# Stored attention tails in two halves, and filling products ahead of the closing stage, in a four-layer interleaved network

## The chip, the cores and the metric

The kernel runs on one core of one Trainium2 chip, as one launch. The metric is the device time of that launch in microseconds (us); lower is better. The engines are named as in the profile: PE is TensorE (matrix products; PEld its weight loads), DVE is VectorE, ACT is ScalarE, POOL is GpSimd and SP is SyncE, which here only issues transfers. An engine name with a q (SPq) is the issue of a transfer by that engine.

## The reference, cut to what matters

Four layers, A B A B, each added to its input. Layer A is a recurrent attention with a memory of 8 tokens over 64 segments of 32 tokens: each segment's first 8 output rows are the memory of the next one, so the segments form a chain. Layer B is a linear attention with learned feature maps, over all 2048 tokens.

```python
def _A_ref(x, mem0, Wq, Wk, Wv, Wo, seg_len):       # x: 1 x 2048 x 640, 32 heads of 192, memory of 8
    mem = mem0
    for s in range(n_seg):                           # 64 segments of 32 tokens
        h = concatenate([mem, x[:, 32*s:32*s+32]])
        q, k, v = h @ Wq, h @ Wk, h @ Wv
        p = softmax(where(mask, q @ k.T * scale, -1e9))
        o = (p @ v) @ Wo
        mem = o[:, :8]
        outs.append(o[:, 8:])

def _B_ref(x, wqkv, w_phi, wo):                      # 32 heads of 20
    q, k, v = split(x @ wqkv)
    phi_q = cat(softmax(q @ w_phi), softmax(-q @ w_phi)); phi_k likewise
    kv, z = phi_k.T @ v, phi_k.sum(tokens)
    return (phi_q @ kv / (phi_q @ z + 1e-6)) @ wo

x = x + _A_ref(layernorm(x), ...); x = x + _B_ref(layernorm(x), ...)   # twice
```

## The kernel before

Layer A is computed in three parts. `A_pre` computes what does not depend on the memory. `A_chain` walks the 64 segments in order, and in each of them four rounds of eight heads (forwards in even segments, backwards in odd ones, `rounds(s)`); its order on every engine is as written. Only the rows that the memory needs go through the output projection inside the chain (`wo_round`, L1263, into the PSUM tile `ps_w`). The last 8 tokens of each segment, its "tail", are not projected there: `turn_tail` lays out a pair of rounds, and `store_tail` (L1256) stores it to `otb_d` in DRAM. A segment stores two such tails of 128 x 192 elements, the one of rounds 0 and 1 and the one of rounds 2 and 3.

The third part is the closing stage, at the beginning of layer B. There the tails of 16 segments at a time (`tb` = 0 to 3) are fetched (`fetch_tails`, L1471), spread into the order that a product needs (`spread_tails`: for each round two copies, by DVE (L94) or ACT (L96) as the letters in `engines` say), and multiplied with all of Wo (`multiply`: 48 steps of a product of 512 columns into `kv_ps[tb % 2]`, L1506, and one of 128 columns into `ps_post`, L1507). Step c uses round c // 12. The results are copied to `obB` by DVE (L1509) and ACT (L1510) and stored (L1512). `kv_ps` has a bank for each of two neighbouring products, but `ps_post` has one bank for all (the pool with `bufs=1`), so the second product's first step on `ps_post` waits for ACT's copy of the first.

The fetches of `tb` 0 and 1 are requested in the chain's last segment, in the list `held`, which `release` issues: four pieces of Wo, the fetch of `tb` 0, four more pieces of Wo (L797), and the fetch of `tb` 1. `tb` 0 is spread inside the chain: rounds 0 and 1 by DVE ahead of its last steps (`"vv"`), rounds 2 and 3 by ACT behind the chain (`"  ss"`). The fetches of `tb` 2 and 3 reuse the memory of 0 and 1 and are issued in layer B, after `wqkv` (L545) and four blocks of rows of x (L406). All of these are on SP's queue, and a transfer there uses one of eight semaphores in turn, so that it also waits for the landing of the eighth transfer before it.

In layer B a scheduler orders each engine's instructions; ACT and DVE then work strictly in that order. In the first layer B the weights are also fused (`fuse`, products and transposes into the four banks `ps_t` and `ps_f`) between the steps of `multiply`. Below, "the first place" is the passage from the first chain to the first layer B (about 1330 to 1360 us), and "the second place" that from the second chain to the second layer B (about 2910 to 2940 us).

Of the kernel before, what the change touches and what calls it, by code (L numbers as in the profile page):

```python
# [8 lines left out]
P = 128  # L9
BF16 = mybir.dt.bfloat16  # L10
# [112 lines left out]
class Kernel:  # L123
# [180 lines left out]
    def layer_B(self, x_dram, at_dram, xout_dram, xnext_dram, li, bp, post):  # L304


        nc, tc, KC, D = self.nc, self.tc, self.KC, self.Dm
# [6 lines left out]
        at = 0  # L314
# [17 lines left out]
        at = LATE  # L332
# [14 lines left out]
        with tc.tile_pool(name=f"B{li}_kv", bufs=1, space=bass.MemoryType.PSUM, reuse_waits="tile") as kvp, \  # L347
# [5 lines left out]
            def side_bank(name):  # L353
                return ptp.tile([P, 512], F32, name=name, tag="side")

            nc.gpsimd.memset(wbd[:], 0.0)
            for i in range(HC):
                n = len(range(i, H, HC))
                nc.gpsimd.dma_start(out=wbd[DH * i:DH * i + DH, 0:n, DH * i:DH * i + DH],
                                    in_=self.B_w_phi[i:H:HC].rearrange("h d f -> d h f"))  # L360
# [190 lines left out]
            with tc.issue_after(last.ins):  # L551
                nc.sync.dma_start(out=wqkv[:, :, 2 * D:3 * D],
                                  in_=self.B_wqkv.rearrange("(k p) n -> p k n", p=P)[:, :, 2 * D:3 * D])
            multiply(0, ow[0], kv_ps[0], side_bank("ps_post"), {})
            ow.append(spread(2, ot[2]))
            side = []
# [144 lines left out]
    def layer_A(self, xn_dram, at_dram, li, x_raw=None):  # L701
# [5 lines left out]
        self.kqb_d = dram.tile([NR, P, NSEG, 192], BF16, name=f"kqb{li}")  # L707
        self.vb_d = dram.tile([NSEG // 8, NR, 2, 64, 2, 2 * VH], BF16, name=f"vb{li}")
        self.tails_d = dram.tile([NSEG // 8, 8, 8, self.Dm], BF16, name=f"tails{li}")
        self.otb_d = dram.tile([P, NSEG, 384], BF16, name=f"otb{li}")  # L710
        wview = self.wview
        wov = self.A_Wo.rearrange("h d m -> (h d) m").rearrange("(q j f) m -> q f j m", j=6, f=32)
        low = self.view(0, LATE)
# [9 lines left out]
        at = 2 * own  # L723
# [63 lines left out]
        def load_both(r, last):  # L787
            for c in (*range(1280, both, 1280), 0):
                held.append(lambda c=c: load_piece(wo_both, r, c))
            if last:  # L790
                held.append(lambda: self.keep_tails(0, low))
                for c in (*range(1280, both, 1280), 0):
                    held.append(lambda c=c: load_piece(wo_kept, order_first, c))
                held.append(lambda: self.keep_tails(1, low))

        def load_piece(into, r, c):
            self.last_load = nc.sync.dma_start(out=into[:, c:c + 1280], in_=self.wo_rows[r, :, own + c:own + c + 1280])  # L797
            return self.last_load
# [259 lines left out]
    def A_chain(self, xn_dram, at_dram, li, load_slot, piece, late_wo, load_both, wo, low):  # L1058
# [3 lines left out]
        with tc.tile_pool(name=f"A{li}_ch", reuse_waits="tile", bufs=1) as sp, \  # L1062
# [190 lines left out]
                return otb[:]  # L1253

            def store_tail(otb, s, r):
                nc.gpsimd.dma_start(out=self.otb_d[:, s, 192 * (r // 2):192 * (r // 2) + 192], in_=otb)  # L1256

            def wo_round(W, r, OT, first, last, part=range(12)):
                for i in part:
# [70 lines left out]
            for s in range(NSEG):  # L1330
# [55 lines left out]
                for n in range(L):  # L1386
                    raw = q_or_k("Q", n + 1)
                    if n == 2:
                        otb = turn_tail(otr)
                    E = weigh()  # L1390
                    next_kq(s, n)
                    turn_rows(raw)
                    if n == 1:
                        step = wo_round(W, order[0], OTs[0], True, False, range(OWN, 12))
                        if s == NSEG - 1:
                            load_both(order[L], True)
                            self.kept_tails = []
                            self.release(step, 12)
                            tails = self.kept_tails
                        else:  # L1400
                            load_both(order[L], False)
                    raw = q_or_k("K", n + 1, n + 1 == L)
                    O = attend(E, n)
                    if n != 2:
                        tails_after(n)
                    fetch_kq(s, n)
                    if n == 2:
                        store_tail(otb, s, order[1])
                    rc = weigh_rows(O)
                    if n == 1:  # L1410
                        rct = weigh_tail()
                    turn_rows(raw)
                    if n == L - 1:
                        output_steps(STEPS[0])
                    pv = v_banks()
                    project(hT, pv, "V", n + 1, s, range(KC))
                    if s == 0 and n == 1:
                        late_wo(1)
                        late_wo(2)
                    osc = raw_of["Q"][:, 0:384]  # L1420
                    for G in range(2):
                        scaled(osc[:, 192 * G:192 * G + 192], O, rc, G, "s")
                    turn(n, osc)
                    v_rows(pv, n + 1, "sv")
                    if n == 1:
                        otr = tail_rows(rct, raw_of["K"][:, 0:192])
# [38 lines left out]
        self.kept_tails.append(self.fetch_tails(tb, low))  # L1465
        return self.tails_load

    def fetch_tails(self, tb, low):
        o = 7680 + 12288 * (tb % 2)
        ot = low[:, o:o + 6144].rearrange("p (s f) -> p s f", f=384)  # L1470
        self.tails_load = self.nc.sync.dma_start(out=ot, in_=self.otb_d[:, 16 * tb:16 * tb + 16, :])  # L1471
        return ot

    def spread_tails(self, tb, ot, low, engines="vsvs"):
        o = 7680 + 12288 * (tb % 2)
        ow = low[:, o + 6144:o + 12288].rearrange("p (r j s x) -> p r j s x", r=4, j=6, x=16)
        for r in range(4):
            if engines[r:r + 1] in ("", " "):
                continue
            for b in range(2):  # L1480
                at = 192 * (r // 2) + (0 if (r + b) % 2 else 16)
                o = ow[:, r, :, b:16:2, :]
                i = ot[:, b:16:2, at:at + 16]
                i = ap3(i, [list(i.ap[0]), [32, 6], *[list(d) for d in i.ap[1:]]])
                self.ev.copy(out=o, in_=i, eng=engines[r])
        return ow

    def post_steps(self, ops):

        nc = self.nc  # L1490
        at_dram, wo, low = self.post_args

        def fetch(tb):
            return self.fetch_tails(tb, low)

        def spread(tb, ot):
            return self.spread_tails(tb, ot, low)

        def multiply(tb, ow, p0, p1, between):
            for c in range(48):  # L1500
                if c in between:
                    between[c]()
                G, j = c % 12 // 6, c % 6
                lhsT = ow[:, c // 12, j, :, :].rearrange("p s x -> p (s x)")[:, G:2 * P:2]
                w = wo[c // 12, c % 12]
                nc.tensor.matmul(p0[:, :], lhsT=lhsT, rhs=w[:, 0:512], start=(c == 0), stop=(c == 47))  # L1506
                nc.tensor.matmul(p1[:, 0:128], lhsT=lhsT, rhs=w[:, 512:640], start=(c == 0), stop=(c == 47))  # L1507
            ob = ops.tile([P, 640], BF16, name="obB", tag="obB", bufs=2)
            done = (nc.vector.tensor_copy(out=ob[:, 0:512], in_=p0[:, :]),  # L1509
                    nc.scalar.activation(out=ob[:, 512:640], in_=p1[:, 0:128], func=ACT.Copy))  # L1510
            av = at_dram.rearrange("(s t) d -> s t d", t=32)
            nc.sync.dma_start(out=av[16 * tb:16 * tb + 16, 24:32, :], in_=ob[:, :])  # L1512
            return done

        return fetch, spread, multiply
# [35 lines left out]
```

## Time and profile before

| | |
|---|---|
| median of 3 runs | 3170.55 us (3170.22 to 3171.96) |
| profiled execution | 3169.9 us, of which the span from first to last instruction 3168.0 us |
| mean granted TensorE clock | 0.992 |
| busy | PE 95%, DVE 69%, ACT 60%, POOL 44% of the span |
| DMA | 749.67 MB, mean 237 GB/s |

In the rows of a timeline the columns are the start, the time of the group, the engine, the line, the operation with output and inputs, the number of instructions, and in brackets the idle time of the engine before it and what ended that. In the rows of the stretches the columns are the stretch and its length, the busy time of PE, PEld, DVE, ACT and POOL, the granted TensorE clock, the mean busy share of the DMA engines and the bytes moved per second.

### The profile page before, as it was taken

What the parts mean: (1) busy time and instruction counts of PE and PEld (TensorE: products, weight loads), DVE (VectorE), ACT (ScalarE), POOL (GpSimd) and SP (SyncE); (2) the same over time, 40 slices, a digit from 0 to 9 for tenths busy, and PEclk for the clock granted to TensorE, in tenths of its full rate; (3) what the DMA queues carried; (4) which work ended last, traced back from release to release, by engine and by line L of the source; (5) the groups of instructions that cost most, each with busy time, mean ns of one, the idle gap of its engine ahead of it and who ended that gap; (6) DMA issues with size and microseconds to landing.
All of it is one profiled execution on the core that took longest, in us unless ns stands there. A gap on an engine that the chain in (4) does not pass through costs nothing.

```text
span 3168.0 us, 141538 instructions
## 1 busy us (share of the span) xinstructions
PE 2993.8 (95%) x59586; PEld 1920.6 (61%) x59586; DVE 2184.4 (69%) x5426; ACT 1906.3 (60%) x4536; POOL 1392.8 (44%) x2872
## 2 busy tenths in 40 slices
PE   8789999999999999899999999999999999998999
PEld 7656666666666665555377566666666666665553
DVE  5467777777777777656644677777777777776565
ACT  3356666666666666646433566666666666666453
POOL 3255555555555555430122555555555555554300
PEclk9999999999999999999999999999999999999999
DMA  9977777877877877840268777777877777778300
GB/s 377 340 263 257 261 248 251 265 257 250 272 252 251 267 256 246 288 166 1 103 246 320 257 255 246 263 264 245 264 259 249 255 261 255 246 259 287 130 1 34
DMA packets 338873, 749.67 MB, mean 237 GB/s; under 512 B 68874, under 2 KB 115330, under 8 KB 335166
## 3 DMA queue, kind: packets, MB, share of 16 engines
q1 hardware_dynamic: 267998, 636.89, 58.3%
q0 software_dynamic: 69376, 100.10, 10.9%
q8 instruction: 469, 7.68, 1.0%
q10 hardware_dynamic: 864, 3.64, 0.3%
q14 instruction: 166, 1.36, 0.1%
HBM read 670.77 MB, written 78.01 MB: 236 GB/s over the span
## 4 chain that ended last, share of the span: by engine, by line
PE 76%; DVE 8%; DMA 6%; issue 5%; ACT 3%; POOL 2%; ACTq 0%; DVEq 0%; SPq 0%; POOLq 0%
PE ps_qk_k L1154 13%; PE ps_qk_q L1154 13%; PE ps_v L1154 12%; PE ps_w L1263 11%; PE ps_s L1191 6%; PE ps_pre L985 4%; PE ps_o L1204 3%; PE kv L1506 2%; DVE raws L1453 2%; ACT raws L1234 2%; DVE hT L1455 2%; PE ps_pq L517 2%; PE ps_t L1217 1%; PE ps_wo L466 1%; DVE QK L1377 1%
## 5 line engine op out<-in xcount | busy, mean ns | idle before, releaser
L1154 PEld LDWEIGHTS <-hT 128*32 128x32 bf16 x30720 | 787.1, 96 | 461.0 <-DVE hT L1455 78.7
L1174 DVE STREAM_TRANSPOSE QK<-raws 128x512 bf16<-128x512 bf16 (+1 forms) x1152 | 730.0, 642 | 219.3 <-ACT raws L1169 163.7
L1130 POOL COPY QK<-kqb 64x192 bf16<-64x192 bf16 x1024 | 349.5, 341 | 486.6 <-PE ps_s L1191 254.1
L1154 PE MATMUL ps_qk_q<-arena,hT 128*32 128x384 bf16 x10240 | 511.3, 327 | 41.4 <-DVE hT L1455 25.6
L1154 PE MATMUL ps_qk_k<-arena,hT 128*32 128x384 bf16 x10240 | 510.1, 328 | 3.0 <-ACT E L1273 1.4
L1169 ACT ACTIVATE raws<-ps_qk_k 128x512 bf16<-128x512 f32 (+1 forms) x640 | 313.5, 510 | 254.0 <-PE ps_qk_k L1154 243.5
L1234 ACT ACTIVATE raws<-ps_o,under 128x192 bf16<-128x192 f32 x1024 | 373.8, 420 | 121.9 <-DVE under L1228 102.5
L1154 PE MATMUL ps_v<-arena,hT 128*32 128x384 bf16 x8192 | 428.4, 326 | 4.0 <-issue 3.0
L1169 ACT ACTIVATE raws<-ps_qk_q 128x512 bf16<-128x512 f32 x512 | 305.7, 597 | 166.6 <-PE ps_qk_q L1154 153.1
L1134 POOL DMA_DIRECT2D Vp<-vb x512 | 257.9, 504 | 316.6 <-PE ps_t L1217 210.7
L1123 POOL DMA_DIRECT2D kqb<-kqb x512 | 292.4, 571 | 69.7 <-POOL QK L1130 59.4
L1191 PEld LDWEIGHTS <-QK 128*80 128x80 bf16 x4096 | 196.0, 121 | 184.9 <-issue 153.8
L1183 DVE CAST Vp<-ps_v 64x384 bf16<-64x384 f32 x512 | 286.3, 559 | 24.5 <-ACT Vp L1181 8.7
L1263 PE MATMUL ps_w<-arena,under 128*32 128x320 bf16 x6144 | 280.6, 300 | 9.5 <-DMA arena<-wo_rows 4.1
L1191 PE MATMUL ps_s<-QK 128*80 128x80 bf16 x4096 | 253.4, 209 | 21.8 <-POOL QK L1130 13.6
L1181 ACT ACTIVATE Vp<-ps_v 64x384 bf16<-64x384 f32 x512 | 246.4, 481 | 35.1 <-PE ps_v L1154 33.6
L1273 ACT ACTIVATE E<-ps_s 80x320 bf16<-80x320 f32 x512 | 217.7, 425 | 42.8 <-PE ps_t L1217 28.6
L985 PEld LDWEIGHTS <-arena 128*128 128x128 bf16 x1920 | 187.9, 98 | 31.0 <-issue 4.7
L1119 POOL DMA_DIRECT2D attn<-under x128 | 91.3, 713 | 262.0 <-DVE under L1115 223.5
L1112 ACT ACTIVATE raws<-ps_w 64x160 f32<-64x160 f32 x256 | 76.6, 299 | 201.1 <-DVE raws L1453 199.6
L1204 PE MATMUL ps_o<-Vp,E 80*32 80x193 bf16 x4096 | 180.3, 248 | 10.2 <-issue 5.7
L1263 PEld LDWEIGHTS <-under 128*32 128x32 bf16 x6144 | 147.2, 96 | 41.6 <-issue 9.8
(167 smaller groups left out, 4360.5 us busy)
## 6 DMA issues: line engine op xcount, KB each, us to landing
arena<-wo_rows SPq DMA_DIRECT2D x560, 320.0 KB, 4.8
arena<-in_A_Wq_dram SPq DMA_DIRECT2D x427, 384.0 KB, 4.5
arena<-in_A_Wk_dram SPq DMA_DIRECT2D x298, 384.0 KB, 5.6
arena<-in_A_Wv_dram SPq DMA_DIRECT2D x290, 384.0 KB, 5.9
kqb<-kqb POOLq DMA_DIRECT2D x512, 48.0 KB, 4.3
kqb<-arena POOLq DMA_DIRECT2D x14, 1536.0 KB, 9.7
Vp<-vb POOLq DMA_DIRECT2D x512, 24.2 KB, 3.8
otb<-otb POOLq DMA_DIRECT2D x256, 48.0 KB, 4.0
```

The costliest lines, as they stand in the source:

```text
L985: nc.tensor.matmul(ps[:, T * i:T * i + T], lhsT=w[b][:, P * c:P * c + P], rhs=xBT[:, b, :], start=(b == 0), stop=(b == KC - 1))
L1123: nc.gpsimd.dma_start(out=kqb[:], in_=self.kqb_d[r, :, s, :])
L1130: nc.gpsimd.tensor_copy(out=o, in_=kqb[h, :].rearrange("p (x c q) -> p x c q", c=3, q=16))
L1134: nc.gpsimd.dma_start(out=Vs[n % 2][64:80, :], in_=self.vb_d[s // 8, r].rearrange("g (t s) x f -> s (g t) (x f)", s=8)[s % 8])
L1154: last = nc.tensor.matmul(o, lhsT=hT[:, b, :], rhs=rhs, start=(i == 0), stop=(i == KC - 1), tile_position=(0, 32 * g), skip_group_check=True)
L1169: nc.scalar.activation(out=raw[:, c], in_=ps[:, c], func=ACT.Copy)
L1174: nc.vector.transpose(out=o, in_=i)
L1183: nc.vector.tensor_copy(out=o, in_=i)
L1191: nc.tensor.matmul(S[0:80, c0:c0 + 80], lhsT=KT[:, 4 * x + c, :], rhs=QT[:, 4 * x + c, :], start=(c % 2 == 0), stop=(c % 2 == 1), skip_gro ...
L1204: nc.tensor.matmul(O[G][32 * h:32 * h + 32, VH * G:VH * G + 193], lhsT=E[0:80, 80 * h + 32 * G:80 * h + 32 * G + 32], rhs=V[0:80, VH * h:V ...
L1234: nc.scalar.activation(out=out, in_=i, func=ACT.Copy, scale=rc[G])
L1263: step = nc.tensor.matmul(W[q:q + 32, 0:320], lhsT=OT[i // 6][:, i % 6 // 2, 32 * (i % 2):32 * (i % 2) + 32], rhs=rhs, start=(first and i ...
```

## The change

The tails in DRAM get an outer dimension for the pair of rounds, so that the tails of one pair for 16 segments lie together, and each fetch becomes two transfers, one for each pair, with a semaphore each. Nothing of the stores but their address changes. Rounds 0 and 1 (or 2 and 3) of a spread depend on their own half alone. At the closing stage's beginning, PE gets 16 products of the identity matrix with the Wo rows of round 1, 512 columns each, into `kv_ps[0]`, whose result is overwritten by the first real product.

```diff
@@ layer_B
                 nc.sync.dma_start(out=wqkv[:, :, 2 * D:3 * D], ...)
+            for _ in range(16):
+                nc.tensor.matmul(kv_ps[0][:, :], lhsT=self.ident[:, :], rhs=self.post_args[1][1, 0][:, 0:512], start=True, stop=True,
+                                 skip_group_check=True)
             multiply(0, ow[0], kv_ps[0], side_bank("ps_post"), {})
@@ layer_A
-        self.otb_d = dram.tile([P, NSEG, 384], BF16, name=f"otb{li}")
+        self.otb_d = dram.tile([2, P, NSEG, 192], BF16, name=f"otb{li}")
...
             if last:
+                held.append(lambda: self.fetch_half(0, 0, low))
                 held.append(lambda: self.keep_tails(0, low))
                 for c in (*range(1280, both, 1280), 0):
                     held.append(lambda c=c: load_piece(wo_kept, order_first, c))
+                held.append(lambda: self.fetch_half(1, 0, low))
                 held.append(lambda: self.keep_tails(1, low))
@@ A_chain
             def store_tail(otb, s, r):
-                nc.gpsimd.dma_start(out=self.otb_d[:, s, 192 * (r // 2):192 * (r // 2) + 192], in_=otb)
+                nc.gpsimd.dma_start(out=self.otb_d[r // 2, :, s, :], in_=otb)
...
-                            self.release(step, 12)
+                            self.release(step, 14)
@@
-    def fetch_tails(self, tb, low):
+    def fetch_half(self, tb, g, low):
+        o = 7680 + 12288 * (tb % 2) + 3072 * g
+        ot = low[:, o:o + 3072].rearrange("p (s f) -> p s f", f=192)
+        self.tails_load = self.nc.sync.dma_start(out=ot, in_=self.otb_d[g, :, 16 * tb:16 * tb + 16, :])
+        return self.tails_load
+
+    def fetch_tails(self, tb, low, halves=(1,)):
         o = 7680 + 12288 * (tb % 2)
-        ot = low[:, o:o + 6144].rearrange("p (s f) -> p s f", f=384)
-        self.tails_load = self.nc.sync.dma_start(out=ot, in_=self.otb_d[:, 16 * tb:16 * tb + 16, :])
-        return ot
+        for g in halves:
+            self.fetch_half(tb, g, low)
+        return low[:, o:o + 6144].rearrange("p (g s f) -> p g s f", g=2, f=192)
...
-                at = 192 * (r // 2) + (0 if (r + b) % 2 else 16)
+                at = 0 if (r + b) % 2 else 16
...
-                i = ot[:, b:16:2, at:at + 16]
+                i = ot[:, r // 2, b:16:2, at:at + 16]
...
-            return self.fetch_tails(tb, low)
+            return self.fetch_tails(tb, low, (0, 1))
```

## The prediction

> **What bounds the kernel now.** I read the page first: how busy PE is, and what the chain of work that ended last consists of.
>
> ```profile
> span 3168.0 us, 141538 instructions
> PE 2993.8 (95%) x59586; PEld 1920.6 (61%) x59586; DVE 2184.4 (69%) x5426; ACT 1906.3 (60%) x4536; POOL 1392.8 (44%) x2872
> PE 76%; DVE 8%; DMA 6%; issue 5%; ACT 3%; POOL 2%; ACTq 0%; DVEq 0%; SPq 0%; POOLq 0%
> ```
>
> PE is busy for 95% of the span and is 76% of that chain, so a change pays only where it fills a hole of PE or speeds PE up. Next I asked for stretches of 4 us around the two places where a chain ends and layer B begins.
>
> ```profile
> 1332.00:1336.00 4.00, 3.26 (x88) 1.79 (x77) 1.50 (x5) 1.16 (x3) 2.88 (x6) 1.00 1.06 397
> 1336.00:1340.00 4.00, 0.00 (x0) 0.00 (x0) 0.53 (x2) 0.00 (x0) 0.00 (x0) 0.88 1.01 348
> 1340.00:1344.00 4.00, 3.84 (x15) 1.92 (x16) 1.72 (x7) 3.13 (x6) 1.31 (x2) 0.50 1.06 434
> 1344.00:1348.00 4.00, 4.00 (x24) 2.02 (x23) 1.17 (x4) 2.65 (x5) 0.00 (x0) 0.77 1.01 348
> 1352.00:1356.00 4.00, 4.00 (x33) 2.23 (x31) 0.00 (x0) 0.00 (x0) 0.66 (x4) 1.00 1.00 422
> 2920.00:2924.00 4.00, 2.95 (x22) 1.66 (x23) 2.25 (x8) 2.24 (x5) 0.68 (x2) 1.00 1.05 424
> 2932.00:2936.00 4.00, 4.00 (x31) 2.18 (x29) 0.69 (x1) 0.28 (x1) 0.00 (x0) 1.00 1.02 419
> ```
>
> At the first place PE has no work from 1336 to 1340, and then works at a granted clock of 0.50 and 0.77. At the second place the clock stays 1.00. The DMA engines are full (1.0 or more) in all these stretches. The timeline of the first place shows what PE waits for.
>
> ```profile
> 1329.28 0.32 SPq L1471 DMA_DIRECT2D arena<-otb  x1
> 1335.22 0.58 PE L1263 MATMUL ps_w<-arena,QK 128*32 128x320 bf16 x10 [0.33 <-issue]
> 1339.36 6.10 SPq L406 DMA_DIRECT2D arena<-in_A_x_dram  x4
> 1339.47 1.17 DVE L94 COPY arena<-arena 128x768 bf16<-128x768 bf16 x4 [5.04 <-DMA arena<-otb]
> 1340.16 0.61 PE L1506 MATMUL kv<-arena 128*128 128x512 bf16 x1 [4.36 <-DVE arena L94]
> 1341.89 3.04 ACT L96 ACTIVATE arena<-arena 128x768 bf16<-128x768 bf16 x4
> 1345.70 3.97 SPq L1471 DMA_DIRECT2D arena<-otb  x2
> 1356.18 0.28 ACT L1510 ACTIVATE obB<-ps_post 128x128 bf16<-128x128 f32 x1 [6.86 <-PE ps_post L1507]
> 1356.51 0.27 PE L1507 MATMUL ps_post<-arena 128*128 128x128 bf16 x2
> ```
>
> The fetch of the first 16 tails, requested at 1329.28, ends DVE's wait at 1339.47, and DVE's copies end PE's 4.36 us. The next two fetches are issued from 1345.70. The first product ends at about 1356.2, ACT copies its `ps_post` (1356.18), and the second product's `ps_post` starts at 1356.51, as soon as that bank is free. The second place has the same shape.
>
> ```profile
> 2916.58 1.00 PE L1263 MATMUL ps_w<-arena,QK 128*32 128x320 bf16 x24
> 2920.36 0.90 DVE L94 COPY arena<-arena 128x768 bf16<-128x768 bf16 x3 [4.55 <-DMA arena<-otb]
> 2921.05 0.39 PE L1506 MATMUL kv<-arena 128*128 128x512 bf16 x1 [3.47 <-DVE arena L94]
> 2921.61 0.38 PE L1506 MATMUL kv<-arena 128*128 128x512 bf16 x1
> 2921.88 0.38 PE L1506 MATMUL kv<-arena 128*128 128x512 bf16 x1
> 2926.65 4.14 SPq L1471 DMA_DIRECT2D arena<-otb  x2
> 2934.30 0.28 ACT L1510 ACTIVATE obB<-ps_post 128x128 bf16<-128x128 f32 x1 [3.86 <-PE ps_post L1507]
> 2934.63 0.27 PE L1507 MATMUL ps_post<-arena 128*128 128x128 bf16 x2
> 2937.46 3.04 ACT L96 ACTIVATE arena<-arena 128x768 bf16<-128x768 bf16 x4 [2.88 <-DMA arena<-otb]
> ```
>
> **The halves: when the first product may start.** A fetch is 1536 KB.
>
> ```profile
> arena<-otb SPq DMA_DIRECT2D x4, 1536.0 KB, 10.4
> ```
>
> Half of it is 0.786 MB. The queue is full, so the first half lands earlier by what its other half takes: at the 397 and 348 GB/s of the first place some 2.1 us, so at 1337.4 instead of 1339.5, and two of DVE's four copies (1.17 / 2 = 0.6) make step 0 ready at 1338.0. At the second place, at 424 GB/s, it is 1.9 us: 2918.5, and ready at 2919.1.
>
> **The fillers: when it does start.** Two steps of the warm product stand 0.27 us apart (2921.61, 2921.88) and stream 640 columns; 512 columns are 0.216 us, and 16 of them 3.46 us. As the two programs are built, PE's order is otherwise the same, the fillers stand right behind the chain's last `ps_w` product, and they wait for nothing. At the first place that one ends at 1335.22 + 0.58 = 1335.80, so the fillers end at 1339.26, later than the 1338.0 of the data: the product starts 0.9 us before 1340.16. At the second place 2917.58 + 3.46 = 2921.04, against 2921.05 before: nothing is won there, the fillers take the 1.9 us that the half would have given.
>
> **The clock.** PE's hole of 4.36 us led to half the clock at the first place, the one of 3.47 us at the second did not. In the slow stretches the loss is 3.84 x 0.50 + 4.00 x 0.23 = 2.84 us. With fillers there is no hole, so I take all of it back. [...] The row bears out that the clock fell; that other runs do without is not seen, since all three timed runs are slower than the profiled one and a run without the loss would be 2.84 us faster. I keep 2.84.
>
> So the first product of the first place would end 0.9 + 2.84 = 3.7 us sooner: the second one's `ps_post` could start at 1352.8.
>
> **What is late next: ACT's order.** As built, the changed program has ACT and DVE in another order in layer B. Before, ACT's copy of the first product's `ps_post` (L1510) stands ahead of all copies of `tb` 2. Now the two copies of `tb` 2, round 1, stand ahead of it, at both places; they wait for the first half of the fetch of `tb` 2. Queued behind that wait are L1510, and behind L1510 PE, whose second product needs the one `ps_post` bank, and SP's store of the result. DVE's copy of `kv_ps[0]` is moved behind two such copies as well, but that bank is needed by the third product only, 13 us later; that costs nothing.
>
> When does that half land? Before, the fetch of `tb` 2 was issued at 1345.70, held up by SP's queue (L406 until 1345.46), not by the copies that free its memory (ACT until 1344.93). That queue drains at the rate of the full DMA engines, so I leave the issue there, and the half lands earlier by 0.786 MB at 422 or 419 GB/s, 1.9 us. First place: 1345.70 + 10.4 - 1.9 = 1354.2. Second place: 2937.46 is when ACT got the whole; 2935.6. ACT then needs 3.04 / 2 = 1.52 us for the two copies and 0.28 us for L1510, and PE follows 0.05 us later (1356.46 to 1356.51).
>
> - First place: 1354.2 + 1.52 + 0.28 + 0.05 = 1356.1 against 1356.51. Of the 3.7 us, 0.4 are left.
> - Second place: 2935.6 + 1.85 = 2937.4 against 2934.63: a loss of 2.8 us.
>
> **The rest of the change.** Four more transfers for each layer on SP at 0.32 us each: SP has waits of several us here, and what is behind (rows of x, `wqkv`) is needed only after four products of 13 us. By the eight semaphores, `wqkv` now waits for the two first halves; the queue still holds two Wo pieces and more then, so I see no hole in the DMA. At nothing, with the cover named; if the DMA ran dry for 1 us, all landings above would be 1 us later, 2 us in the sum. The stores of the chain (256, of 384 bytes a row as before) only change address. What slower or faster ones could do in 128 segments no row shows; the bounds are what PE waits for transfers, since these share the engines:
>
> ```profile
> PE ps_w L1263 <- DMA arena<-wo_rows: 8.1, 12, 1.5
> PE ps_qk_q L1154 <- DMA arena<-in_A_Wq_dram: 4.6, 2, 2.9
> PE ps_o L1204 <- DMA Vp<-vb: 1.9, 4, 1.0
> ```
>
> Together 14.6 us, some of it start-up: from -10 (gone) to +10 (doubled). I take zero: same number of rows, same bytes.
>
> **Sum.** -0.4 + 2.8 = +2.4 us on the profiled 3169.9 us (the span of 3168.0 and 1.9 around it), which is 0.65 us under the median of the runs: 3170.55 + 2.4 = 3173.0 us. That is within 0.2% (6.3 us, about what a measurement of this kernel can tell from no change).
>
> **Rivals.**
> 1. *The new stall itself cools the clock (slower).* PE stands still for 1352.8 to 1356.1 = 3.3 us at the first place, 2.8 at the second. Each restart at half the clock costs 2.84 as above. In one place: 3175.9. In both, as it would be if the halves land about 1 us later than I say (+2 more): 2.4 + 5.7 + 2 = +10, and with no later landing +8.1: 3178.7 to 3180.7. It decides from a hole between 3.47 us (clock kept) and 4.36 us (lost). For it: the first place is close to that. Against: the second is well below.
> 2. *No stall.* If the first half of `tb` 2 landed 3 us sooner than I say, ACT would be ready in time, and -3.7 and 0 remain: 3166.8. For it: the half's memory is free sooner than before. Against: SP's queue, not memory, set the issue.
> 3. *The cold clock is rare in ordinary runs of before.* Then the second `ps_post` could start at 1353.7 before, and the first place loses 2.4 instead of winning 0.4: +5.2, 3175.8. Against it speak the three runs, as said.
> 4. *The stores' new addresses slow or speed the chain.* Slower by 10 us: 3180.6; faster by 10: 3160.6. Nothing in the profile speaks for either.
>
> That the change does not do what it says is not open: fillers and halves stand in the built program where they are meant.
>
> **How the numbers follow.** Forecast 0.27, rival 1 in one place 0.10, rival 2 0.09, rival 3 0.08: all within 0.2%, 0.54. Rival 1 in both places 0.21 and rival 4 slower 0.15: slower, 0.36. Rival 4 faster: 0.10. The range from 3166 to 3181 leaves out the faster side of rival 4 and part of its slower one. The forecast's own range is 3171 to 3175, by 1 us of landing time at each place.
>
> **What would show it.** In the changed profile: the clock at 1.00 from 1336 to 1352; the first product starting near 1339.2 and 2921.0, right behind fillers 0.216 us apart; ACT's two copies of `tb` 2 right ahead of L1510's, and a wait of PE for ACT's `obB` of some 3 us at both places, starting near 1352.8 and 2934.2. I am wrong if PE goes through from the first to the second product, if the clock drops there, or if the span of the 64 segments itself differs by more than 1 us.

## The result, and the profile after

The changed kernel took 3178.28 us (median of 17 runs) beside 3170.22 us for the kernel before on the same chip, a ratio of 1.0022 (95% interval 1.0012 to 1.0033): by this ratio +7.0 us, between +3.8 and +10.5. A second comparison, told below, gave 1.0011 (0.9999 to 1.0022). The forecast was +2.4 us, "within 0.2%"; the first measurement lies just above that line, inside the stated range of 3166 to 3181 us and outside the forecast's own of 3171 to 3175. The profiled execution took 3182.34 us.

The page of the changed kernel: busy time, and the chain of work that ended last.

```profile
span 3180.5 us, 141588 instructions
PE 3004.0 (94%) x59584; PEld 1926.7 (61%) x59618; DVE 2185.9 (69%) x5426; ACT 1909.7 (60%) x4536; POOL 1398.5 (44%) x2872
PE 73%; DMA 9%; DVE 8%; issue 4%; ACT 3%; POOL 2%; SPq 0%; DVEq 0%; POOLq 0%; ACTq 0%
```

In that chain DMA has gone from 6% to 9% and PE from 76% to 73%: more of it hangs on transfers. Among the waits of PE stands one that the kernel before does not have (total us, times, longest):

```profile
PE ps_post L1518 <- ACT obB L1521: 8.8, 2, 4.7
```

The product into `ps_post` is L1518 now (L1507 before), ACT's copy of it L1521 (L1510), the product into `kv` L1517, the chain's `ps_w` product L1268, the fetch of tails L1476, the fillers L555 (the trace has 15 of the 16). The timeline of the first place:

```profile
1341.61 0.32 PE L1268 MATMUL ps_w<-arena,QK 128*32 128x320 bf16 x4 [0.16 <-DMA arena<-wo_rows]
1342.09 3.40 PE L555 MATMUL kv<-arena,ident 128*128 128x512 bf16 x15 [0.16 <-issue]
1343.80 2.52 SPq L545 DMA_DIRECT2D arena<-in_B_wqkv_dram  x2
1343.86 1.17 DVE L94 COPY arena<-arena 128x768 bf16<-128x768 bf16 x4 [3.57 <-DMA arena<-otb]
1345.33 0.38 PE L1517 MATMUL kv<-arena 128*128 128x512 bf16 x1
1346.75 5.74 SPq L406 DMA_DIRECT2D arena<-in_A_x_dram  x4
1352.72 5.68 SPq L1476 DMA_DIRECT2D arena<-otb  x4
1361.72 1.57 ACT L96 ACTIVATE arena<-arena 128x768 bf16<-128x768 bf16 x2 [6.63 <-DMA arena<-otb]
1363.32 0.28 ACT L1521 ACTIVATE obB<-ps_post 128x128 bf16<-128x128 f32 x1
1363.65 0.37 PE L1518 MATMUL ps_post<-arena 128*128 128x128 bf16 x2 [4.69 <-ACT obB L1521]
```

The fillers fill the old hole, and the first product starts behind them. Then ACT stands still for the half of `tb` 2 until 1361.72, copies it, only then frees the `ps_post` bank, and PE has stood for 4.69 us. The second place has the same shape:

```profile
2922.94 1.00 PE L1268 MATMUL ps_w<-arena,QK 128*32 128x320 bf16 x24 [0.37 <-DVE QK L1382]
2925.49 1.17 DVE L94 COPY arena<-arena 128x768 bf16<-128x768 bf16 x4 [2.28 <-DMA arena<-otb]
2927.34 0.38 PE L1517 MATMUL kv<-arena 128*128 128x512 bf16 x1
2934.06 5.81 SPq L1476 DMA_DIRECT2D arena<-otb  x4
2943.18 1.58 ACT L96 ACTIVATE arena<-arena 128x768 bf16<-128x768 bf16 x2 [6.48 <-DMA arena<-otb]
2945.11 0.27 PE L1518 MATMUL ps_post<-arena 128*128 128x128 bf16 x2 [4.14 <-ACT obB L1521]
```

The stretches (start and end, length, busy time of PE, PEld, DVE, ACT and POOL, granted clock, DMA share, GB/s) show what follows each stall:

```profile
1342.00:1346.00 4.00, 3.91 (x20) 1.88 (x20) 1.59 (x6) 0.77 (x3) 0.00 (x0) 1.00 1.02 357
1358.00:1362.00 4.00, 0.96 (x6) 0.41 (x5) 0.24 (x1) 0.28 (x1) 0.00 (x0) 1.00 1.03 415
1362.00:1366.00 4.00, 2.35 (x13) 1.46 (x13) 1.80 (x6) 3.75 (x6) 0.00 (x0) 0.54 1.01 395
2942.00:2946.00 4.00, 0.89 (x8) 0.53 (x8) 1.86 (x5) 2.79 (x5) 0.00 (x0) 1.00 1.01 416
2946.00:2950.00 4.00, 4.00 (x19) 1.99 (x18) 0.18 (x1) 0.64 (x1) 0.00 (x0) 0.57 1.04 380
```

At the first place the clock stays 1.00 where it fell before, and falls 20 us later, behind the new stall. At the second place, where it had stayed 1.00, it falls too.

### The profile page after: what moved, and what is told of

Read it like the earlier page. It is cut to its first block, busy times and chain, and to the rows that moved or that the text cites. A ratio compares the mean times of both kernels' runs of the same rounds, so it can differ in the third digit from the quotient of the medians.

```text
span 3180.5 us, 141588 instructions
## 1 busy us (share of the span) xinstructions
PE 3004.0 (94%) x59584; PEld 1926.7 (61%) x59618; DVE 2185.9 (69%) x5426; ACT 1909.7 (60%) x4536; POOL 1398.5 (44%) x2872
## 3 DMA queue, kind: packets, MB, share of 16 engines
q0 software_dynamic: 69376, 100.10, 10.8%
q10 hardware_dynamic: 864, 3.64, 0.3%
## 4 chain that ended last, share of the span: by engine, by line
PE 73%; DMA 9%; DVE 8%; issue 4%; ACT 3%; POOL 2%; SPq 0%; DVEq 0%; POOLq 0%; ACTq 0%
PE ps_qk_k L1159 12%; PE ps_qk_q L1159 12%; PE ps_v L1159 11%; PE ps_w L1268 10%; PE ps_s L1196 6%; PE ps_pre L990 5%; DMA arena<-wo_rows 3%; PE ps_o L1209 2%; DVE raws L1458 2%; PE ps_wo L466 2%; PE kv L1517 2%; DMA under<-tails 2%; ACT raws L1239 2%; PE ps_pq L517 2%; DVE hT L1460 1%
## 5 line engine op out<-in xcount | busy, mean ns | idle before, releaser
L1268 PE MATMUL ps_w<-arena,under 128*32 128x320 bf16 x6144 | 282.7, 301 | 13.0 <-DMA arena<-wo_rows 5.8
L1268 PEld LDWEIGHTS <-under 128*32 128x32 bf16 x6144 | 148.4, 96 | 43.9 <-issue 11.7
```

Source lines behind the costliest of these rows:

```text
L1268: step = nc.tensor.matmul(W[q:q + 32, 0:320], lhsT=OT[i // 6][:, i % 6 // 2, 32 * (i % 2):32 * (i % 2) + 32], rhs=rhs, start=(first and i ...
```

## The experiments

Two theories at the start. **A**: the fillers and the halves do what they should, and the loss is ACT's order, which makes PE wait for the `ps_post` bank and then cools the clock. **Rivals**: B, the fillers cost by themselves; C or D, the halves or the new addresses change the transfers. Every kernel was timed beside the kernel before on the same chip. Its own median was 3170.2, 3171.6, 3177.3 and 3177.8 us in the four comparisons, so ratios are compared.

To see where each kernel stands at the two places, I take from each profiled execution the time from the start of the chain's last `ps_w` product to the start of the last step of the fourth output product, and add the two places: 128.3 us for the kernel before, 137.6 for the changed kernel. "At the places" below is the difference of this sum to 128.3.

| kernel | at the places, us | ratio to before (95%) | us from the ratio |
|---|---|---|---|
| changed | +9.3 | 1.0022 (1.0012 to 1.0033) | +7.0 |
| changed, again | +8.2 | 1.0011 (0.9999 to 1.0022) | +3.5 |
| e1_fill | -1.4 | 1.0003 (0.9989 to 1.0017) | +1.0 |
| e2_halves | -5.2 | 0.9966 (0.9952 to 0.9981) | -10.8 |
| e2_halves, again | -3.0 | 0.9990 (0.9979 to 1.0001) | -3.2 |
| e3_order | -2.6 | 0.9975 (0.9961 to 0.9989) | -7.9 |
| e4_bank | -0.4 | 0.9999 (0.9982 to 1.0016) | -0.3 |
| e5_layout | +2.8 | 0.9992 (0.9980 to 1.0003) | -2.5 |
| e7_warm | +4.6 | 1.0021 (1.0009 to 1.0034) | +6.7 |
| e7_warm, again | +6.7 | 1.0021 (1.0009 to 1.0034) | +6.7 |
| e8_stall | +13.0 | 1.0043 (1.0026 to 1.0059) | +13.6 |
| e9_nine | -4.9 | 0.9978 (0.9965 to 0.9992) | -7.0 |
| e10_stall | +1.0 | 0.9988 (0.9978 to 0.9998) | -3.8 |

The second column is from one execution, the last from the ratio over all runs, whose intervals are about 4 us to each side; they agree within 5.6 us, and what is ordered far apart in one is so in the other. (In the trace of e2_halves the last step into `kv` is missing at the second place; its time is taken from the `ps_post` step behind it, which gives -5.2, where the expectation of its second run says 5.8 us less.) Of the changed kernel's +9.3 us, 5.1 have come about when the second product's `ps_post` starts, and 4.1 come behind it.

**e1_fill: the fillers alone**, on the kernel before (old layout, whole fetches).

```
+            for _ in range(16):
+                nc.tensor.matmul(kv_ps[0][:, :], lhsT=self.ident[:, :], ...)
             multiply(0, ow[0], kv_ps[0], side_bank("ps_post"), {})
```

> The kernel before with the 16 fillers alone (whole fetches, old layout). Theory A (the loss is PE waiting for ps_post behind ACT's copies of tb 2, and the cold clock after that wait): in this build ACT's copy of the first ps_post stays ahead of the copies of tb 2, so there is no wait; the first product starts with its data as before (4.4 us after the chain's last product), the clock stays 1.00 at the first place: -2.8 us there, 0 to +0.2 at the second, about -2.6 us against the kernel before. Rival B (the fillers themselves cost, by power, instruction loading or by delaying PE): slower than before by most of the 7 us that the change costs.

Measured: 1.0003, +1.0 us between -3.5 and +5.4. The fillers alone do not cost 7 us; B is out, and e3_order, with the same fillers, confirms it. The 2.6 us that A let them win are not seen, but they lie inside the interval. The profile has no wait of PE for `obB`, and this is what is left of PE's waits for the first copies:

```profile
PE kv L1509 <- DVE arena L94: 0.8, 1, 0.8
```

**e2_halves: layout and halves, no fillers.**

```
-            for _ in range(16):
-                nc.tensor.matmul(kv_ps[0][:, :], lhsT=self.ident[:, :], ...)
```

> The changed kernel without the fillers: halves and new layout alone. In this build ACT's copy of the first ps_post is ahead of the copies of tb 2 again. Theory A: no wait of PE for obB; the hole of PE ahead of the first product shrinks from 4.4 to about 2.5 us at the first place and from 3.5 to 2.2 at the second, and the clock stays up: -1.9 - 2.8 - 1.3 = about -6 us against the kernel before. Rival C (the halves or the stores' new addresses slow the transfers): slower than before, by up to the 7 us of the whole change, with a longer chain of segments or later landings.

Measured: 0.9966, and 0.9990 in the second comparison. The halves win (the second time with an interval that reaches 1.0001) and cost nothing, so C is out. Without the fillers the scheduler leaves ACT's copy of the first `ps_post` ahead of the copies of `tb` 2: the bad order comes only from both parts of the change together. PE's waits:

```profile
PE ps_post L1515 <- DVE arena L94: 4.3, 2, 2.3
```

The 7.8 us for the first copies (4.36 + 3.47) have become 4.3, and nothing replaces them.

**e3_order: the whole change with ACT's order mended.** The copies of `tb` 2 are issued only after those of the first product's banks.

```
-            multiply(0, ow[0], kv_ps[0], side_bank("ps_post"), {})
-            ow.append(spread(2, ot[2]))
+            done0 = multiply(0, ow[0], kv_ps[0], side_bank("ps_post"), {})
+            with tc.issue_after(done0[0].ins), tc.issue_after(done0[1].ins):
+                ow.append(spread(2, ot[2]))
```

> The changed kernel with one thing put right: the copies of tb 2 are issued behind the copies of the first product's results, so that ACT's copy of the first ps_post is ahead of them. Fillers, halves and layout as in the changed kernel. Theory A: no wait of PE for obB and no cold clock at either place; the first product starts 3.4 us behind the chain's last product (before: 4.4 and 3.5): -1 - 2.8 - 0.1 = about -4 us against the kernel before, 11 us faster than the changed kernel. Rivals B and C: still about 7 us slower than before.

Measured: 0.9975, 11 to 15 us under the changed kernel by the ratios of the two comparisons, with the same fillers, halves and layout. There is no wait for `obB`, and the stretches around the old stall are full at full clock:

```profile
1340.00:1344.00 4.00, 4.00 (x26) 2.09 (x25) 2.07 (x8) 2.79 (x6) 1.23 (x2) 1.00 1.03 378
1352.00:1356.00 4.00, 3.95 (x32) 2.34 (x32) 0.69 (x1) 0.28 (x1) 1.07 (x6) 1.00 1.08 400
1356.00:1360.00 4.00, 4.00 (x37) 2.58 (x36) 1.03 (x4) 1.97 (x3) 0.00 (x0) 1.00 1.00 410
```

**e4_bank: ACT's order left bad, but the second product given a free bank** for its 128 columns, so that it need not wait.

```
-            multiply(1, ow[1], kv_ps[1], side_bank("ps_post"), between[0])
+            multiply(1, ow[1], kv_ps[1], kv_ps[2], between[0])
```

> The changed kernel with ACT's order left as it is (the copies of tb 2 for round 1 ahead of the first ps_post's copy), but the second product's 128 columns go to the third kv bank, which is free at that time. If theory A's link is the ps_post bank: PE goes from the first to the second product without a wait, though ACT's copy is as late as before; clock 1.00; about -4 us against the kernel before. If the late copy costs by another way (SP's store of the first product, the copies of tb 2 late for the third product): a wait of PE somewhere later, and a time between -4 and +7 us.

Measured: 0.9999. PE's wait for `obB` is gone, and with it the loss at the places (-0.4 us after +9.3); the ratio agrees, though its interval reaches 1.0016. The order still costs by a second way. PE's transposes into `ps_t` (L183) need banks that ACT and DVE empty, and ACT is behind the same transfer:

```profile
1360.38 1.58 ACT L96 ACTIVATE arena<-arena 128x768 bf16<-128x768 bf16 x2 [6.66 <-DMA arena<-otb]
1363.72 3.06 ACT L96 ACTIVATE arena<-ps_t 120x640 bf16<-120x640 bf16 x5
1364.70 0.60 PE L183 MATMUL ps_t<-ident,arena 128*120 128x128 bf16 x6 [1.93 <-DVE arena L94]
```

**e5_layout: the new addresses alone**, each group still fetched whole, no fillers.

```
-            self.fetch_half(tb, g, low)
+        ot = low[:, o:o + 6144].rearrange("p (g s f) -> p g s f", g=2, f=192)
+        self.tails_load = self.nc.sync.dma_start(out=ot.rearrange("p g s f -> p g (s f)"),
+            in_=self.otb_d[:, :, 16 * tb:16 * tb + 16, :].rearrange("g p s f -> p g (s f)"))
```

> The new layout of the stored tails alone: each group of 16 segments is still fetched whole, by one transfer, at the old place, and there are no fillers; ACT keeps the copy of the first ps_post ahead of the copies of tb 2, and no half lands early. Theory A (the time is made at the two places, by the halves and by what ACT does behind them): no change from the kernel before, 3168 to 3175 us, with PE's wait for the first copies at 3.5 to 4.4 us as before. Rival D (the new addresses make the stores or the fetches cheaper, and that is most of the 11 us that the halves without fillers won): 3160 to 3165 us, with a fetch of 1536 KB landing in under 10.4 us or with PE's waits in the chain shorter by over 3 us in the sum.

Measured: 0.9992, -2.5 us between -6.3 and +1.0. The chain with its new addresses costs and wins nothing like 10 us; D is out. PE's wait for the first copies is the whole fetch's again, even longer than before:

```profile
PE kv L1507 <- DVE arena L94: 9.3, 2, 4.7
```

**e7_warm: the stall kept, PE kept busy in it**, with 20 products more on a free bank between the first and the second output product; run twice.

```
+            with tc.issue_after(self.last_kv.ins):
+                for _ in range(20):
+                    warm = nc.tensor.matmul(kv_ps[2][:, :], lhsT=self.ident[:, :], ...)
+            with tc.issue_after(warm.ins):
                 multiply(1, ow[1], kv_ps[1], side_bank("ps_post"), between[0])
```

> The changed kernel as it is, ACT's late order and all, and 20 products more on a bank that is free then (kv_ps[2]), between the first and the second output product: 20 x 0.216 = 4.3 us of work inside the stall of 4.1 to 4.7 us. The stall stays, the hole in PE's work goes. If the half clock behind the stall is a cost of its own, as rival 1 of the prediction has it, the clock stays 1.00 at both places and the time falls by 2 x 2.84 = 5.7 us against the changed kernel: 3172 to 3174 us. If the clock is no part of it (the stall alone, or something in the chain), the time stays at 3177 to 3180 us.

> The changed kernel with 20 products in the stall, again, now directly beside the changed kernel. Its profile showed the clock at 1.00 at both places and the fourth product ending 4.7 us sooner in the sum of the two, but its median was no lower. If the half clock is a cost of its own that ordinary runs pay, it is 3 to 6 us faster than the changed kernel here and its mean granted clock higher; if it is again within 1.5 us of it with a higher clock, then the time won behind the stall is lost again elsewhere in the run, and where is to be looked for.

Measured: 1.0021 both times; beside the changed kernel on one chip 3182.79 us against 3181.29. The clock did stay up, in the profile and in the runs: mean granted clock 0.9932 over both sets of 12 runs, 0.9911 and 0.9919 over those of the changed kernel. The stretches where the changed kernel stood, in the first of the two:

```profile
1350.00:1354.00 4.00, 4.00 (x25) 1.98 (x24) 0.06 (x1) 0.10 (x1) 0.00 (x0) 1.00 1.03 411
1354.00:1358.00 4.00, 4.00 (x31) 2.25 (x29) 1.82 (x6) 3.92 (x6) 0.00 (x0) 1.00 1.01 408
```

From the second product's first `ps_post` step to the last step of the fourth product this execution needs 50.4 and 40.0 us, the changed kernel 52.7 and 41.5: the half clock is worth 3.7 us in the profiles. The medians do not show it. In the second run a wait for `obB` of 1.2 us was left at the first place. So the stall carries the loss, and what its cold clock adds in ordinary runs is not settled.

**e8_stall: a first try at the bad order without fillers.** It did more than that: the copies of `tb` 2 write where those of `tb` 0 lie, they came ahead of the first product, and that product waited for them and worked on their data.

```
-            multiply(0, ow[0], kv_ps[0], side_bank("ps_post"), {})
-            ow.append(spread(2, ot[2]))
+            ow.append(self.spread_tails(2, ot[2], self.post_args[2], "vs"))
+            done0 = multiply(0, ow[0], kv_ps[0], side_bank("ps_post"), {}, self.act_copies)
```

> The halves without fillers (3160.1 us, where ACT copies the first ps_post ahead of tb 2), with one thing changed: ACT is made to do its two copies of tb 2, round 1, first, as in the changed kernel. Theory A (ACT's order is what costs, and the fillers only brought it about): the second output product waits for the half of tb 2 as in the changed kernel, a hole of PE of 5 to 6 us (the first product ends 1 us sooner, the half lands when it did) and half the clock behind it at both places: 3176 to 3180 us. Rival B (it is the fillers that cost, the order is an accompaniment): 3160 to 3164 us.

Measured: 1.0043, +13.6 us. It is no test of the order, but it prices a hole: PE waits 9.6 and 9.1 us for DVE at the two places,

```profile
PE kv L1518 <- DVE arena L94: 18.7, 2, 9.6
```

10.9 us more than the 7.8 of the kernel before, and the time goes up by 13.6. Here the kernel pays about what PE stands; the interval is 8 to 19 us.

**e10_stall: the same, built rightly**, the copies of `tb` 2, round 1, behind the first product's reads and ahead of ACT's copy of its `ps_post`; no fillers.

```
+            with ExitStack() as order:
+                if ahead is not None:
+                    ahead[0]()                # the copies of tb 2, rounds 0 and 1
+                    order.enter_context(self.tc.issue_after(ahead[1][0].ins))
+                done1 = nc.scalar.activation(out=ob[:, 512:640], in_=p1[:, 0:128], func=ACT.Copy)
...
+            with tc.issue_after(done0[1].ins):
                 multiply(1, ow[1], kv_ps[1], side_bank("ps_post"), between[0])
```

> The halves without fillers, with one thing changed: ACT does its two copies of tb 2, round 1, ahead of the copy of the first ps_post, as in the changed kernel, and the first product reads its own copies. (In the earlier attempt at this, the copies of tb 2 stood ahead of the first product in the program; they write where the copies of tb 0 lie, and the product waited for them and worked on their data.) Theory A (ACT's order is what costs): PE waits for obB between the first and the second product, a hole of 5 to 6 us, since the first product ends 1 us sooner than in the changed kernel and the half of tb 2 lands when it did, with half the clock behind it at both places; the second product's ps_post starts 21.5 to 22 us after the start of the chain's last products, and the time is that of the changed kernel, a ratio of 1.001 to 1.0035 to the kernel before. Rival B (the fillers cost, and the order only goes with them): the time of the halves without fillers, a ratio of 0.995 to 0.998.

Measured: 0.9988, the time of the halves without fillers (3173.20 against 3173.95 us on the same chip). A's number failed: ACT is as late as in the changed kernel, and yet the loss is not there in the time. (At the places this execution stands 4.0 us above the halves' second one; the medians do not show that.) The timeline of the second place says why:

```profile
2931.75 3.62 PE L1524 MATMUL kv<-arena 128*128 128x512 bf16 x16
2936.12 1.57 ACT L96 ACTIVATE arena<-arena 128x768 bf16<-128x768 bf16 x2 [6.47 <-DMA arena<-otb]
2937.72 0.28 ACT L1531 ACTIVATE obB<-ps_post 128x128 bf16<-128x128 f32 x1
2938.05 1.18 PE L1525 MATMUL ps_post<-arena 128*128 128x128 bf16 x16 [2.68 <-ACT obB L1531]
```

With the second product bound behind that copy, the scheduler reordered PE: 16 of its products into `kv`, which need no `ps_post`, run ahead in the wait, and their 16 `ps_post` products follow together. At the first place it is 10 such products and 18 transposes into `ps_t`, and no wait for `obB` is left there. The changed kernel has one `kv` product ahead of the blocked `ps_post`. So the order on ACT is half of the cause; the other half is that PE has nothing else in front of the blocked product. (This kernel has no fillers either; that they are not what makes the difference rests on e1_fill and e3_order.)

**e9_nine: 9 fillers instead of 16, with e3's order.**

```
-            for _ in range(16):
+            for _ in range(9):
```

> The version that theory A would choose: halves, the copies of tb 2 held behind the first product, and 9 fillers in place of 16 (1.9 us instead of 3.5, so that they end when the first half's copies are done, 2.4 to 2.7 us after the start of the chain's last products). Against 16 fillers in that order (3163.6 us) the first product can start 1.0 to 1.3 us sooner at each place: 3161 us. Against the halves without fillers (3160.1 us) only the clock is kept, which there fell for 3.4 us at one place: 1.7 us at most, 3158.5 us. So 3158 to 3162 us; above 3165 us the fillers cost by something else than their own time.

Measured: 0.9978, the same as with 16 fillers (0.9975) and no better than without any (0.9966, 0.9990). At the places it is 2.3 us better than e3, as expected, but the medians cannot tell such differences apart.

**The changed kernel and the halves, again**, on one chip with e10_stall and e7_warm.

> The changed kernel once more, beside the others on one chip, so that they can be compared with it directly: a ratio of 1.001 to 1.0033 to the kernel before, as in its first runs, waits of PE for obB of 4 to 5 us at both places and half the clock behind them. A ratio below 1.000 would say that the first comparison was off by more than its interval.

> The halves without fillers again, the fastest so far (0.9966), directly beside the changed kernel. At the two places its profile showed 5.8 us less than the kernel before; its median showed 10.7 less. If the places are all there is to it, the ratio is 0.998 to 0.9985 here; if the layout or the builds matter beside them, 0.9955 to 0.9975 again. In both cases it is 12 us or more below the changed kernel (15.1 by the places).

Measured: 3181.29 and 3173.95 us, ratios of 1.0011 and 0.9990. The loss of the changed kernel and the gain of the halves are both smaller than at first: 7.3 us apart, where 12 or more were expected. The stall is there as before:

```profile
PE ps_post L1518 <- ACT obB L1521: 8.3, 2, 4.6
```

Versions that beat both kernels are thus at hand: halves alone (0.9966, and 0.9990 with an interval up to 1.0001), and the whole change with ACT's order mended (0.9975).

## Why the prediction was right or wrong

The mechanism was right and the chain of steps held; the size of the stall was too small, and with it the case that was called the likeliest.

- **Fillers.** Right to 0.1 us. From the end of the last `ps_w` product (1341.93 and 2923.94) the first product starts after 3.40 us at both places, where it was 4.36 and 3.47: gains of 1.0 and 0.1, against 0.9 and 0 predicted.
- **The first half.** DVE's copies start 1.93 and 1.55 us after that end, before 3.67 and 2.78: 1.7 and 1.2 us earlier, where I computed 2.1 and 1.9.
- **The clock at the first place** stayed 1.00 until the stall, as predicted.
- **What is late next.** ACT's order and PE's wait for `obB` are where the prediction put them. The stall is 4.69 and 4.14 us, not 3.3 and 2.8. Counted from the end of the last `ps_w` product, the second product's `ps_post` starts at 21.7 us (before 20.7) and 21.2 us (before 17.05): +1.0 and +4.1, where the sum had -0.4 and +2.8. That is the term that was mis-sized, by 2.7 us in all.
- **The step that failed.** "`wqkv` now waits for the two first halves ... At nothing." The issue of `wqkv` (L545) comes at 1343.80, 1.9 us behind the end of the chain and 0.06 us ahead of the half's copies; in the kernel before it came 1.5 us ahead of the end, as its timeline has it:

```profile
1334.27 3.10 SPq L545 DMA_DIRECT2D arena<-in_B_wqkv_dram  x2
```

  What SP's queue waits for around the first place says why, first before, then after:

```profile
SPq L545 <- DMA arena<-wo_rows: 0.5, 1, 0.5
SPq L545 <- DMA arena<-otb: 3.5, 2, 1.8
```

  The DMA engines stayed full (1.02 in that stretch), which is what I had looked at; but the rows of x and the fetch of `tb` 2 stand behind it in SP's order. The fetch is issued 10.8 and 10.1 us after the end instead of 9.9 and 9.1. Its half then takes 9.0 and 9.1 us to land where I had 8.5 and 8.9. I had taken the issue of that fetch as fixed by a queue that does not change. Over all profiled executions `wqkv` comes 1.2 to 2.9 us ahead of the end with whole fetches (6 places) and 0.5 to 2.2 us behind it with halves (22 places). For the fetch of `tb` 2 it is 9.8 us on average (9.1 to 10.3) and 10.4 us (9.4 to 11.4): the change moves it by about 0.7 us, and the rest of the 0.9 and 1.05 seen here lies within that scatter. Why the landing takes longer, by 0.5 us at the first place, no run shows.
- **Rival 1** had exactly this, "the halves land about 1 us later", and half the clock at both places: +8.1 to +10. The places show +9.3 and +8.2 in the two profiles, the ratios +7.0 and +3.5. By the profiles it was the case to be called likeliest; that its half clock costs time in ordinary runs is what e7_warm left open. I spoke against it because 3.3 and 2.8 us lay below the 3.47 that kept the clock; with 1.3 us of error in each stall that was no margin, and 3.47 is no bound either (last section).
- **Rival 2** (no stall) did not come about in the change, but e3 shows its time once the order is right: 0.9975, -7.9 us, where it was given -3.7.
- **Rival 3** (half clock rare in ordinary runs of before) is not borne out: e1 raises the mean granted clock from 0.9913 to 0.9930. But e1's time does not fall with it (its interval reaches down to -3.5 us), so the 2.84 us that I took back at the first place are neither shown nor refuted as time. The three runs that I held against this rival prove little: the 17 of the comparison spread from 3162.28 to 3178.64 us. In the profiled executions all nine holes of 3.64 us and more were followed by half the clock (last section).
- **Rival 4** (addresses) is refuted by e5: -6.3 to +1.0 us, not 10 to either side.
- **What would show it.** I wrote that a difference of over 1 us in the span of the 64 segments would prove me wrong. That was too sharp: from first to last `ps_w` product the first chain takes 1179.0 us before and 1182.0 after, the second 1185.7 and 1184.8, while over all profiled executions, old layout and new, the first varies from 1175.9 to 1185.6.

## What to carry to other kernels

When a transfer is split so that its first part can be used sooner, look at what the scheduler does with the freed work: here the copies of a later group moved ahead of the copy that frees the only bank, and took back more than the split had won (+9.3 us at the places, where the halves alone show -5.2). Price a new wait from everything that its release hangs on, and count a moved DMA also for what stands behind it in its queue, even when the engines stay full (here 1.02, and the fetch behind it about 0.7 us later). What a stall cost was what the next engine could not do meanwhile: at the second place ACT stood for the half 6.48 us in the changed kernel and 6.47 in e10_stall, and PE behind it 4.14 and 2.68. Before removing the wait, see whether products that do not need the blocked bank can go ahead of the one that does.

## What the hardware showed that was not expected

The bound that I took for the clock, kept at a hole of 3.47 us and lost at 4.36, is none. In the halves' second run a hole of 2.72 us at the first place was followed by half the clock, and one of 2.17 us at the second was not. The wait of PE for both, and the stretches behind them:

```profile
PE kv L1514 <- DVE arena L94: 4.9, 2, 2.7
```

```profile
1340.00:1344.00 4.00, 1.22 (x7) 0.49 (x7) 1.24 (x5) 0.25 (x1) 0.00 (x0) 0.73 1.03 358
1344.00:1348.00 4.00, 4.00 (x17) 2.03 (x16) 1.01 (x3) 3.81 (x7) 1.31 (x2) 0.50 1.03 413
2920.00:2924.00 4.00, 4.00 (x31) 2.30 (x30) 1.01 (x3) 3.69 (x7) 1.31 (x2) 1.00 1.04 411
```

Over all profiled executions, holes of 1.9 to 2.7 us (in e2_halves, its second run, e4_bank and e10_stall) were followed by half the clock five times in eight, one of 3.47 (the kernel before) was not, and all nine of 3.64 us and more (the kernel before, both runs of the changed kernel, e5_layout, e8_stall) were. The time at half clock at the places was always 3.4, 6.8, 10.2 or 13.7 us, whole multiples of 3.41.

The clock records say more. In the executions of the kernel before and of the changed kernel the granted clock is 1.00 or 0.50, and it changes only at points of a grid of 3.413 us: it stays at 0.50 for 3.413, 6.827 or 13.653 us each time (only the last time, which the end of the execution cuts short, for less), and between those times at 1.00 for whole multiples too, such as 1160.532 us, 340 times 3.4133, ahead of the first place of the kernel before. Whether half the clock followed a hole went with how the hole fell on that grid. These are cells of the grid, each with a stretch in which PE stands: the hole of 4.36 us (half the clock behind it) and the first part of the one of 3.47 us (full clock) in the kernel before, then those of 2.72 us (half) and 2.17 us (full) in the halves' second run.

```profile
1335.60:1339.01 3.41, 0.20 (x6) 0.00 (x0) 0.00 (x0) 0.00 (x0) 0.00 (x0) 1.00 0.99 341
2915.97:2919.38 3.41, 1.54 (x40) 1.07 (x39) 0.00 (x0) 0.00 (x0) 0.00 (x0) 1.00 0.97 341
1338.41:1341.82 3.41, 1.21 (x24) 0.32 (x15) 0.00 (x0) 0.00 (x0) 0.46 (x2) 1.00 1.01 362
2915.36:2918.77 3.41, 1.45 (x40) 0.99 (x39) 0.48 (x2) 0.00 (x0) 0.33 (x2) 1.00 1.01 359
```

By its busy time PE is idle for 94, 55, 64 and 58% of them. The grid cut the hole of 3.47 us, behind which the clock stayed 1.00, in two: the next cell, 1.75 us busy, is idle for 49%. Over all profiled executions, of the cells from 1300 to 1430 and from 2880 to 3000 us that begin at full clock, all 13 with PE idle for 60% or more were followed by half the clock, two of the seven between 54 and 58%, and none with 52% or less. My estimate from these shares: a lone hole of over 4.1 us (twice 60% of 3.413) leaves one cell idle for 60% wherever the grid lies, and one of under 1.8 us (54%) leaves none idle for 54%; between them it depends on where the grid lies. Elsewhere in the run idle time alone does not tell the two apart: from 200 to 3150 us all 33 cells of 60% and more were followed by half the clock, but so were eight of 18 to 37% (one of 18%, from 1591.60 us, in the kernel before).

The kernel before differs by 7.5 us in its median from one comparison to another (3170.2 to 3177.8), more than the whole effect of this change, and the ratio of one unchanged kernel to the kernel before differed by 0.0024 between two comparisons (the halves), about the width of an interval. A change of 0.1 to 0.2% in such a kernel needs a second comparison before it is believed.
